# Wider projections, features by minimum, key sums halved on GpSimd, and the last key tile's causal triangle as a minimum on VectorE

## The chip, the cores and the metric

One core of a Trainium2 chip (trn2). The metric is device time of one execution in microseconds. A core has TensorE (PE), VectorE (DVE), ScalarE (ACT), GpSimd (POOL) and SyncE (SP, which here only starts DMAs). They run their own instruction streams in order and wait for each other by semaphores.

## The reference

Four residual blocks over x [2048, 512], 32 heads of 16, all in bfloat16: A, B, A, B with the same weights twice.

```python
x = x + A(layernorm(x)); x = x + B(layernorm(x)); x = x + A(layernorm(x)); x = x + B(layernorm(x))
# A: four segments of 512 tokens, M and z summed over the segments before
a_dot = softmax(q k^T / 4 + causal mask) v          # within the segment
a_mem = (phi(q) M) / (phi(q) z + 1e-6)              # phi(t) = t + 1 where t > 0, else exp(t)
o = g * a_mem + (1 - g) * a_dot                     # g = sigmoid(beta), per head;  then o @ wo
M, z = M + phi(k)^T v, z + sum(phi(k))
# B: linear attention over all 2048 tokens, without a mask
f(t) = concat(softmax(t w_phi), softmax(-t w_phi))  # over 16 features of a head, each sign
o = (f(q) (f(k)^T v)) / (f(q) sum(f(k)) + 1e-6)     # then o @ wo
```

## The kernel before

The program is a graph of operations (`Graph.op`), each with its reads, writes and buffers. The order on every engine, the engine of those operations that may run on two, and the buffer slot of every tile come from a table written into the source (`ORDER`, read by `place`). `emit` writes the five streams in that order with the waits that the graph needs. A new graph therefore has a new table: every engine's order differs.

x stays in SBUF (`X`, 16 tiles of 128 tokens). `ln` normalises a tile: statistics on DVE (L577, L578), the root on POOL (L585, L587; for the first four tiles on ACT), the scaling on DVE (L594, L598), and a transpose, mostly by DMA.

`a_proj` works on a segment. For each of four groups of eight heads it forms K and Q (512 columns each, interleaved, L341) in one PSUM tile `D`, of which there are four, each two banks wide. K is copied to `KT` (tile name `p`), and DVE writes four masked copies of it into `pQ` (L679), which put the heads apart. The feature phi is exp(t) from PSUM on ACT, max(t, 0) (L634) and min(exp, 1) + max (L635) on DVE. V gets a column of ones (`pV`); the weight of V is scaled once by 1/(1 + exp(beta)) on POOL (L530). `pW` is V with the partition halves swapped by DMA.

`a_att` works on two query tiles of a segment. For each group of heads: score products (L326) into PSUM, exponentials on ACT (L351), value products with the exponentials as stationary operand (L326, 17 columns: 16 of V and one for the sum), division (L389, L847), and from the second segment on the memory part (L764) added (L851). Scores of the diagonal tile go to `pF`, those of the last key tile, which only the second query tile sees, to `pE`. In both the causal triangle is one more product that adds -1e9 before the exponential: `tri`, the triangle, by `two`, a doubled identity.

`b_keys` forms exp(k) and exp(-k) (1024 columns on ACT for two token tiles), sums over each head's 16 features on DVE (L945), takes reciprocals, forms V and multiplies it by them straight from PSUM (L973), and adds the products with the keys (L341, `pT`). `b_query` does the queries: denominators (L1018 to L1024), the product with the sums (L1043), the sum of the two signs (L1049), the transposed output. `out_proj` applies wo; x is added by DVE (L898), or for 12 of the 32 tiles of block B by an identity product on PE (`RES_PE`, `D<-X,ident`) with a copy back.

Of the kernel before, what the change touches and what calls it, by code (L numbers as in the profile page):

```python
# [9 lines left out]
ACT = mybir.ActivationFunctionType  # L10
# [72 lines left out]

class Op:
# [5 lines left out]
class Graph:  # L90
# [4 lines left out]
    def _touch(self, o, item, write):  # L95
        if isinstance(item, tuple):
# [201 lines left out]
class Kernel:  # L298
# [97 lines left out]
    def alloc(self):  # L396
# [8 lines left out]
        self.eps6 = sb("eps6", [128, 1], F32)  # L405
        self.two64 = sb("two64", [128, 2, 64], BF16)
# [6 lines left out]
        self.gt = sb("gt", [128, 3, H], F32)  # L413
        self.GAm = sb("GAm", [128, NG, 8, 17], F32)
# [17 lines left out]
        self.pQ = pool("pQ", N_KM, [128, 4, 2, 2, 128], BF16, {}, ("KM",))  # L432
        self.pK = pool("pK", N_QT, [128, 512], BF16, {}, ("QT",))
# [16 lines left out]
    def setup(self):  # L450
# [26 lines left out]
        load(lambda: [(self.beta_sb[:], inp["A_beta"].partition_broadcast(128))], 8, [R("beta")], "pool")  # L477
        load(lambda: [(self.wphi_st[:], inp["B_w_phi"].rearrange("(g hl) d j -> (hl d) g j", g=NG))], 60, [R("wphi")], "pool")
# [34 lines left out]
        for hf in range(2):  # L513
            v(lambda e, hf=hf: e.tensor_copy(self.tri[64 * hf:64 * hf + 64, :], tw.t[64 * hf:64 * hf + 64, 64 * hf:64 * hf + 64]), 100,
              [tw], [R("tri", hf)])
        v(lambda e: e.memset(self.epsln[:], LN_EPS), 70, [], [R("epsln")])
# [4 lines left out]
        v(lambda e: e.tensor_scalar(gt[:, 1, :], gt[:, 0, :], 1.0, None, op0=ALU.add), 100, [R("gt")], [R("gt1")])  # L521
        v(lambda e: e.reciprocal(gt[:, 2, :], gt[:, 1, :]), 270, [R("gt1")], [R("gt2")])
        v(lambda e: e.tensor_tensor(self.GAm[:, :, :, 0:16], gt[:, 0, :, None].to_broadcast([128, H, 16]).rearrange("p (g h) c -> p g h c", g=NG),
                                    self.H8[:, None, :, None].to_broadcast([128, NG, 8, 16]), ALU.mult), 620,
          [R("gt"), R("H8")], [R("GAm")], label="gates")
        v(lambda e: e.tensor_copy(self.GAm[:, :, :, 16], self.H8[:, None, :].to_broadcast([128, NG, 8])), 100,
          [R("H8")], [R("GAm")], label="gates")

        for dt in range(4):
            fn = lambda e, dt=dt: e.tensor_tensor(self.WA["v"][:, dt, :].rearrange("p (h d) -> p h d", h=H),  # L530
                                                  self.WA["v"][:, dt, :].rearrange("p (h d) -> p h d", h=H),
                                                  gt[:, 2, :, None].to_broadcast([128, H, DH]), ALU.mult)
            self.g.op({"dve": (602.0, fn), "pool": (1100.0, fn)}, [R("gt2"), R("WA", "v")], [R("WAv", dt)], label="gate")

        two = lambda fn, a, b: self.g.op({"pool": (a, fn), "dve": (b, fn)}, [], [], label="one", port=True)
        for i, tv in enumerate(self.pV.tensors):
            self.pV.init[i] = two(lambda e, tv=tv: e.memset(tv[:, :, :, 16:17], 1.0), 560.0, 190.0)
# [36 lines left out]
    def ln(self, t, xT, flex=False, pe=False, root="pool"):  # L574
# [15 lines left out]
        if flex:  # L590
            nb = self.nb[:, t:t + 1]
            v(lambda e: e.scalar_tensor_tensor(nb, self.mv[:, t, 0:1], -1.0, rs, op0=ALU.mult, op1=ALU.mult), 70,
              [R("mv", t), R("rstd", t)], [R("nb", t)], label="nb")
# [35 lines left out]
    def phi(self, ps, dst, src=None, c=0):  # L629

        v = self.v
        e_ = self.T(self.p1, "phe")
        self.act(lambda: e_.t[:], lambda: ps.t[:, c:c + 512], ACT.Exp, 512, [ps[c]], [e_], label="phexp")
        v(lambda e: e.tensor_scalar(dst.t[:], src.t[:], 0.0, None, op0=ALU.max), 202, [src], [dst], label="phmax", port=True)  # L634
        v(lambda e: e.scalar_tensor_tensor(dst.t[:], e_.t[:], 1.0, dst.t[:], op0=ALU.min, op1=ALU.add), 335, [dst, e_], [dst], label="phadd", port=True)  # L635


# [20 lines left out]
    def a_proj(self, L, s):  # L658
# [7 lines left out]
        for g in range(NG):  # L666
            ps = self.T(self.pD, "gen")
            if L == 0 and s == 0 and g == 0:
                self.warm()
            KT = self.T(self.p1, "KT")  # L670
            KM = self.T(self.pQ, "KM")
            QT = self.T(self.pK, "QT")
            pk = self.T(self.p1, "phiKT") if s < 3 else None
            PQ = self.T(self.p1, "phiQ") if s >= 1 else None
            self.wproj(ps, (self.WA["k"], self.WA["q"]), [R("WA", "k", g // 2), R("WA", "q", g // 2)], (g, g), xT,
                       opens=[KT, QT] + ([pk] if pk else []) + ([PQ] if PQ else []), label="KQ")
            self.evac(lambda KT=KT: KT.t[:], lambda ps=ps: ps.t[:, 0:512], 512, [ps[0]], [KT], label="Kev")
            for sl in range(4):
                fn = lambda e, KM=KM, KT=KT, sl=sl: e.tensor_scalar(  # L679
                    KM.t[:, :, sl % 2, :, 64 * (sl // 2):64 * (sl // 2) + 64], KT.t[:].rearrange("p (j h k) -> p j h k", j=4, h=2),  # L680
                    self.m4[:, sl:sl + 1], None, op0=ALU.mult)
                self.g.op({"dve": (262.0, fn)}, [KT, R("m4")], [KM[sl]], label="Km", port=True)
            st["KM"].append(KM)
            if pk:
                PK = self.T(self.p1, "PhK")
                self.phi(ps, pk, KT)
                dst = lambda PK=PK: PK.t[:].rearrange("p (a b) -> p a b", a=4)
                if first:
                    self.tpe(dst, lambda pk=pk: pk.t, [pk], [PK], label="PhKtr")
                else:  # L690
                    self.tr(dst, lambda pk=pk: pk.t[:], [pk], [PK], label="PhKtr")
                st["PhK"].append(PK)
            self.evac(lambda QT=QT: QT.t[:], lambda ps=ps: ps.t[:, 512:1024], 512, [ps[512]], [QT], label="Qev")
            st["QT"].append(QT)
            if PQ:
                self.phi(ps, PQ, QT, 512)
                st["PhQ"].append(PQ)
        wv = lambda dt: self.WA["v"][:, dt, :].rearrange("p (k a e) -> p a k e", k=8, a=2)
        for t2 in (0, 2):
            ps = self.T(self.pD, "gen")  # L700
            self.tproj(ps, wv, [R("WAv", i) for i in range(4)], (t2, t2 + 1), lambda tt, dt: xT.t[:, dt, tt * 128:(tt + 1) * 128],
# [66 lines left out]
    def a_att(self, L, s, i0):  # L768
# [11 lines left out]
        for gg in range(2):  # L780
            PV = self.T(self.pD, "pv")
            for g in (2 * gg, 2 * gg + 1):
                KM, QT = st["KM"][g], st["QT"][g]
                rd = [QT] + [KM[sl] for sl in range(4)]
                key = lambda hf, j, p, x, KM=KM: KM.t[64 * hf:64 * hf + 64, j, p, x, :]
                qry = lambda hf, c, n, QT=QT: QT.t[64 * hf:64 * hf + 64, i0 * 128 + c:i0 * 128 + c + n]
                PT, PF = {}, {}
                for j in range(i0 + 1):
# [19 lines left out]
                    (S.t[:, hf * 512 + p * 192 + 64 * (1 - x):hf * 512 + p * 192 + 192 - 128 * x], key(hf, i0 + 1, p, x), qry(hf, 128 + 64 * x, 128 - 64 * x), p + x == 0, False)  # L808
                    for p in range(2) for x in range(2) for hf in range(2)] + [
                    (S.t[:, hf * 512:hf * 512 + 384].rearrange("p (a b) -> p a b", a=2)[:, :, 0:128], two(hf), tri(hf, 4), False, True) for hf in range(2)],  # L810
                    [], rd + trir, [S], opens=[PE], label="Sd", rows=64, dur=286)
                self.act(lambda PE=PE: PE.t[:, :, 64:256], lambda S=S: S.t[:, :].rearrange("p (a b) -> p a b", a=2)[:, :, 0:384].rearrange("p a (c e) -> p a c e", c=2),
                         ACT.Exp, 768, [S], [PE], scale=0.25, label="expd")

# [35 lines left out]
            if s >= 1:  # L850
                v(lambda e, part=part: e.tensor_tensor(part(o), part(o), part(tmp), ALU.add), 335, [o[gg], tmp], [o[gg]], label="oadd", port=True)  # L851
# [70 lines left out]
    def b_keys(self, L, c, parts):  # L922
# [4 lines left out]
        for part in parts:  # L927
            Es, Vts = {}, {}
            units = [part[i:i + 2] for i in range(0, len(part), 2)]
            for u in units:  # L930
# [9 lines left out]
                for sgn in range(2):  # L940
# [3 lines left out]
                             ACT.Exp, 512 * n, [S[0], S[512]][:n], [E[sgn]], scale=1.0 - 2.0 * sgn, label="kexp")  # L944
                    fn = lambda e, sgn=sgn, eo=eo, Z=Z, n=n: e.tensor_reduce(Z.t[:, 0:64 * n].rearrange("p (k s h) -> p k s h", k=n, s=2)[:, :, sgn, :],  # L945
# [11 lines left out]
                if copied:  # L957
# [4 lines left out]
                    for k, tt in enumerate(u):  # L962
                        Vt = Vts[tt]
                        for sgn in range(2):
                            v(lambda e, sgn=sgn, Vt=Vt, vs=vs, k=k: e.tensor_tensor(
                                Vt.t[:, sgn, :, 0:16, :], vs.t[:, k * 512:(k + 1) * 512].rearrange("p (g d h) -> p g d h", g=NG, h=8),
                                Vt.t[:, sgn, :, 16:17, :].to_broadcast([128, NG, 16, 8]), ALU.mult), 335,
                              [vs, Vt[("z", sgn)]], [Vt[("v", sgn)]], label="Vt", port=True)
# [18 lines left out]
    def b_query(self, L, c, store):  # L987
# [13 lines left out]
        zv = lambda s, k: ZQ.t[:, :].rearrange("p (a x) -> p a x", a=2)[:, :, 0:256].rearrange("p a (s k x) -> p a s k x", s=2, k=2)[:, :, s, k, :]  # L1001
# [7 lines left out]
        zr = [ZQ[(gp, sgn)] for gp in range(2) for sgn in range(2)]  # L1009
# [6 lines left out]
        self.act(lambda: u(0), lambda: zv(1, 1), ACT.Ln, 128, zr, [t1[0]], label="zln")  # L1016
# [9 lines left out]
        for tt in range(4):  # L1026
# [21 lines left out]
            if not pair:  # L1048
              v(lambda e, Tm=Tm, o=o: e.tensor_tensor(o.t[:].rearrange("p (a c) -> p a c", a=2), half(Tm, 0), half(Tm, 1), ALU.add), 335, [Tm], [o], label="nadd", port=True)  # L1049
# [8 lines left out]
    def build(self):  # L1058
# [5 lines left out]
        def lnA(L, s):  # L1064
            self.xA[(L, s)] = self.T(self.pX, "xA")
            for t in range(s * 4, s * 4 + 4):
                self.ln(t, self.xA[(L, s)], flex=(L == 1), pe=("xA", L, t) in PE_T, root="act" if L == 0 and s == 0 else "pool")
# [44 lines left out]
N_XT, N_KM, N_K1, N_K2, N_VT, N_SM, N_QT, N_PE, N_PF = 5, 6, 16, 19, 5, 6, 6, 2, 3  # L1112
# [116 lines left out]
```

## Time and profile before

| | before |
|---|---|
| median of 3 runs | 483.18 us (480.74 to 484.05) |
| profiled execution | 480.2 us, span 478.5 us, clock 0.987 |
| busy PE / DVE / ACT / POOL | 95% / 92% / 90% / 12% |

The span is the time from the first to the last instruction of the execution that was profiled. A PE record contains a fixed part beside its streaming, so records overlap and a busy PE is not at its peak. Groups of instructions are named by line, engine and operation, written tile <- read tiles; `p` and `pS` stand for the shared SBUF tiles, `D` for PSUM. A mean duration contains the start of an instruction, which overlaps the one before.

### The profile page before, as it was taken

Reading aid. Unit: us, or ns where it says so; the run is one execution under the profiler, and the core shown is the slowest. Engines: PE = TensorE matmul, PEld = TensorE weight load, DVE = VectorE, ACT = ScalarE, POOL = GpSimd, SP = SyncE. Lnnn points to the kernel's source line nnn. Section 1 sums busy time; section 2 is a strip of 40 time slices with the busy share of each in tenths; the row PEclk is TensorE's granted clock in tenths of the full one; section 3 lists DMA queues with packets and bytes.
Section 4 is the critical chain, followed back from the end, with each engine's and each line's share of the span. In section 5 each row is a group of like instructions: output and inputs, shape, how many; then the busy total and the mean of one; then the engine's idle time right before and its main releaser. Section 6 shows DMA issues by size and latency. Waiting matters only on the chain.

```text
span 478.5 us, 25222 instructions
## 1 busy us (share of the span) xinstructions
PE 454.4 (95%) x11582; PEld 300.5 (63%) x11582; DVE 438.2 (92%) x917; ACT 429.2 (90%) x566; POOL 58.2 (12%) x142
## 2 busy tenths in 40 slices
PE   7999999999999989998999998999999999999895
PEld 3456565757666776666555767676667666666453
DVE  5999999999999989898999999999999998998893
ACT  3799999999999997579999999999999999667892
POOL 2703030200011011100220020210010011110000
PEclk9999999999999999998999999999999999999799
DMA  8562433351536011200233344325113303200346
GB/s 243 142 130 54 72 71 63 76 108 32 60 65 71 20 37 25 47 1 5 36 79 79 62 68 71 57 47 95 27 26 60 47 15 60 37 12 3 47 81 209
DMA packets 89450, 30.36 MB, mean 63 GB/s; under 512 B 76000, under 2 KB 89344, under 8 KB 89344
## 3 DMA queue, kind: packets, MB, share of 16 engines
q1 hardware_dynamic: 88992, 28.46, 31.7%
q8 instruction: 91, 1.49, 1.3%
q10 hardware_dynamic: 288, 0.26, 0.2%
q0 software_dynamic: 64, 0.02, 0.1%
q14 instruction: 15, 0.12, 0.1%
HBM read 6.32 MB, written 2.10 MB: 18 GB/s over the span
## 4 chain that ended last, share of the span: by engine, by line
PE 56%; ACT 30%; DVE 9%; DMA 2%; issue 2%; POOL 1%; DVEq 0%; POOLq 0%
PE D L341 37%; PE D L326 18%; ACT p L351 15%; ACT pF L351 10%; ACT pE L351 4%; DVE stats L577 1%; DMA beta_sb<-in_A_beta_dram 1%; DVE p L764 1%; DVE pQ L679 1%; DVE p L598 1%; DMA p<-p 1%; DVE p L360 1%; PE D L378 1%; ACT pS L351 1%; DVE p L635 1%
## 5 line engine op out<-in xcount | busy, mean ns | idle before, releaser
L351 ACT ACTIVATE p<-D 128x1024 bf16<-128x1024 f32 (+1 forms) x276 | 250.2, 955 | 18.3 <-PE D L341 12.1
L326 PE MATMUL D<-pK,pQ 64*128 64x256 bf16 (+3 forms) x1536 | 114.6, 244 | 6.6 <-ACT p L351 2.8
L351 ACT ACTIVATE pF<-D 128x896 bf16<-128x896 f32 x128 | 117.1, 941 | 2.7 <-PE D L326 2.2
L326 PEld LDWEIGHTS D<-pK,pQ 64*128 64x128 bf16 x1536 | 53.8, 94 | 42.7 <-ACT p L351 11.3
L326 PE MATMUL D<-pV,pF 64*128 64x34 bf16 x1024 | 75.8, 176 | 1.9 <-ACT pF L351 1.1
L326 PE MATMUL D<-pW,pF 64*128 64x34 bf16 x1024 | 73.1, 176 | 0.0
L341 PE MATMUL D<-pX,WA_k 64*128 64x512 bf16 x256 | 65.0, 377 | 0.0
L341 PE MATMUL D<-pX,WA_q 64*128 64x512 bf16 x256 | 65.0, 377 | 0.0
L326 PEld LDWEIGHTS D<-pV,pF 64*128 64x128 bf16 x1024 | 56.2, 93 | 4.7 <-ACT pF L351 2.3
L585 POOL TENSOR_SCALAR rstd<-mv 128x1 f32<-128x1 f32 x60 | 14.6, 244 | 360.2 <-DVE mv L578 358.1
L351 ACT ACTIVATE pE<-D 128x768 bf16<-128x768 f32 x64 | 52.7, 835 | 1.4 <-PE D L326 0.7
L326 PE MATMUL D<-pV,p 64*128 64x34 bf16 x1024 | 52.8, 176 | 0.1
L326 PEld LDWEIGHTS D<-pW,pF 64*128 64x128 bf16 x1024 | 52.2, 93 | 0.8
L326 PE MATMUL D<-pW,p 64*128 64x34 bf16 x1024 | 51.5, 176 | 0.0
L326 PEld LDWEIGHTS D<-pV,p 64*128 64x128 bf16 x1024 | 47.2, 93 | 3.2 <-ACT pE L351 0.3
L326 PEld LDWEIGHTS D<-pW,p 64*128 64x128 bf16 x1024 | 45.5, 93 | 2.5
L326 PE MATMUL D<-tri,two 64*128 64x128 bf16 (+1 forms) x384 | 46.6, 234 | 0.0
L577 DVE BATCH_NORM_STATS2 stats<-X 128x6 f32<-128x512 bf16 x64 | 43.2, 683 | 3.0 <-DMA X<-in_A_x_dram 2.7
L326 PE MATMUL D<-pV,pE 64*128 64x34 bf16 x512 | 45.2, 176 | 0.2 <-issue 0.2
L326 PE MATMUL D<-pW,pE 64*128 64x34 bf16 x512 | 43.3, 176 | 0.0
L679 DVE TENSOR_SCALAR pQ<-p,m 128x512 bf16<-128x512 bf16 x128 | 42.5, 351 | 0.2
L945 DVE TENSOR_REDUCE pS<-p 128x64 f32<-128x1024 bf16 (+1 forms) x36 | 39.0, 1090 | 1.0 <-ACT p L351 1.0
(121 smaller groups left out, 1003.7 us busy)
## 6 DMA issues: line engine op xcount, KB each, us to landing
pW<-pV SPq DMA_DIRECT2D x16, 136.0 KB, 2.6
out_dram<-X SPq DMA_DIRECT2D x7, 256.0 KB, 4.4
X<-in_A_x_dram SPq DMA_DIRECT2D x3, 512.0 KB, 7.1
pX<-in_B_wqkv_dram SPq DMA_DIRECT2D x3, 512.0 KB, 5.5
p<-p SPq DMA_TRANSPOSE x76, 2.5
pX<-p SPq DMA_TRANSPOSE x54, 3.0
WA_q<-in_A_wq_dram SPq DMA_DIRECT2D x2, 256.0 KB, 6.1
WB_o<-in_B_wo_dram SPq DMA_DIRECT2D x8, 64.0 KB, 3.1
```

Source lines behind the costliest of these rows:

```text
L326: ins = e.matmul(out_ap, lhsT, rhs, start=st, stop=sp, tile_position=(basep(lhsT), basep(out_ap)))
L341: ins = e.matmul(out_ap, lhsT[64 * hf:64 * hf + 64], rhs[64 * hf:64 * hf + 64], start=k == 0 and i == 0, stop=k == 1 and i == len(lists[hf ...
L351: return self.g.op({"act": (dur, lambda e: e.activation(out_ap(), in_ap(), func, scale=scale))}, reads, writes, opens, label=label)
L360: "dve": ((340 if fast else n / 0.96 + 65), lambda e: e.tensor_copy(out_ap(), in_ap()))}
L378: ins = e.transpose(pb()[:, k * 128:(k + 1) * 128], src()[:, k * 128:(k + 1) * 128], self.ident[:])
L577: v(lambda e: e.bn_stats(self.stats[:, t, :], self.X[:, t, :]), 602, [R("X", t)], [R("st", t)], label="bn")
L585: v(lambda e: e.tensor_scalar(rs, self.mv[:, t, 1:2], LN_EPS, None, op0=ALU.add), 170, [R("mv", t)], [R("rstd", t)], eng="pool", label="rstd")
L598: v(lambda e: e.tensor_scalar(xn.t[:], self.X[:, t, :], self.mv[:, t, 0:1], self.rstd[:, t:t + 1], op0=ALU.subtract, op1=ALU.mult), 300, [ ...
L635: v(lambda e: e.scalar_tensor_tensor(dst.t[:], e_.t[:], 1.0, dst.t[:], op0=ALU.min, op1=ALU.add), 335, [dst, e_], [dst], label="phadd", po ...
L679: fn = lambda e, KM=KM, KT=KT, sl=sl: e.tensor_scalar(KM.t[:, :, sl % 2, :, 64 * (sl // 2):64 * (sl // 2) + 64], KT.t[:].rearrange("p (j h ...
L764: v(lambda e: e.tensor_tensor(tmp.t[:].rearrange("p (y h r d) -> p y h r d", y=16, h=2, r=2), NM.t[:, :].rearrange("p (h y r d) -> p y h r ...
L945: fn = lambda e, sgn=sgn, eo=eo, Z=Z, n=n: e.tensor_reduce(Z.t[:, 0:64 * n].rearrange("p (k s h) -> p k s h", k=n, s=2)[:, :, sgn, :], eo( ...
```

## The change

- **Projections.** K of two groups (1024 columns) fills a PSUM tile, then Q of the two; copies, masks and features work on 1024 columns. `pQ` and `pK` have half as many tiles of double size; the other pools change in number.
- **Features.** phi = min(exp(t), max(t, 0) + 1); exp reads the copy in SBUF, not PSUM.
- **Gates.** V's weight is no longer scaled. V's extra column is 1 + exp(beta), and the mask of the memory is scaled in place of it.
- **Key sums.** GpSimd halves 16 features to 8 and 8 to 4; DVE sums 4. This is done for the units of two token tiles (28 sums); the 8 of single tiles stay.
- **Values and denominators of B** are copied from PSUM to SBUF first, and the multiplication makes both signs in one instruction.
- **Residual.** All additions of x are on DVE.
- **Triangle.** For `pE` the product with `tri` is gone; after the exponential DVE takes the minimum with `keep`, which is 3e38 where a key is seen and 0 where not. `pF` keeps its product.
- Two sums (L851, L1049) may run on POOL (9 and 16 of 50 do). The loads of beta and w_phi go to the queues of ACT and SP.
- A new order table.

```diff
...
-        self.pQ = pool("pQ", N_KM, [128, 4, 2, 2, 128], BF16, {}, ("KM",))
-        self.pK = pool("pK", N_QT, [128, 512], BF16, {}, ("QT",))
+        self.pQ = pool("pQ", N_KM, [128, 8, 2, 2, 128], BF16, {}, ("KM",))
+        self.pK = pool("pK", N_QT, [128, 1024], BF16, {}, ("QT",))
...
+            fn = lambda e, tv=tv: e.tensor_copy(tv[:, :, :, 16], self.gc[:, None, :].to_broadcast([128, 4, H]))
...
-        self.act(lambda: e_.t[:], lambda: ps.t[:, c:c + 512], ACT.Exp, 512, [ps[c]], [e_], label="phexp")
-        v(lambda e: e.tensor_scalar(dst.t[:], src.t[:], 0.0, None, op0=ALU.max), ...
-        v(lambda e: e.scalar_tensor_tensor(dst.t[:], e_.t[:], 1.0, dst.t[:], op0=ALU.min, op1=ALU.add), ...
+        self.act(lambda: e_.t[:], lambda: src.t[:], ACT.Exp, 1024, [src], [e_], psum=False, label="phexp")
+        v(lambda e: e.tensor_scalar(dst.t[:], src.t[:], 0.0, 1.0, op0=ALU.max, op1=ALU.add), ...
+        v(lambda e: e.tensor_tensor(dst.t[:], e_.t[:], dst.t[:], ALU.min), ...
...
+            self.wproj(ps, (self.WA["k"],) * 2, [R("WA", "k", hp)], gs, xT, opens=[KT], label="KQ")
+            self.evac(lambda KT=KT: KT.t[:], lambda ps=ps: ps.t[:], 1024, [ps[0], ps[512]], [KT], label="Kev")
...
-                    (S.t[:, hf * 512:hf * 512 + 384].rearrange("p (a b) -> p a b", a=2)[:, :, 0:128], two(hf), tri(hf, 4), False, True) for hf in range(2)],
...
+                v(lambda e, PE=PE: e.tensor_tensor(PE.t[:, :, 64:192].rearrange("p a (b c) -> p a b c", b=2), PE.t[:, :, 64:192].rearrange("p a (b c) -> p a b c", b=2),
+                                                   self.keep[:, None, None, :].to_broadcast([128, 4, 2, 64]), ALU.min), 335, ... label="cutd", port=True)
...
+                        self.g.op({"pool": (1160.0, lambda e, e3=e3, s3=s3: e.tensor_tensor(s3(), e3()[:, :, 0:8], e3()[:, :, 8:16], ALU.add))},
+                                  [E[sgn]], [sc], label="zh")
+                        self.g.op({"pool": (770.0, lambda e, s3=s3: e.tensor_tensor(s3()[:, :, 0:4], s3()[:, :, 0:4], s3()[:, :, 4:8], ALU.add))},
+                                  [sc], [sc], label="zh")
...
-N_XT, N_KM, N_K1, N_K2, N_VT, N_SM, N_QT, N_PE, N_PF = 5, 6, 16, 19, 5, 6, 6, 2, 3
+N_XT, N_KM, N_K1, N_K2, N_VT, N_SM, N_QT, N_PE, N_PF = 5, 3, 10, 21, 5, 6, 3, 2, 4
...
-VCOP = set()
+VCOP = {(L, c) for L in range(2) for c in range(4)}
...
-RES_PE = {(0, t) for t in (2, 3, 6, 7)} | {(1, t) for t in (2, 3, 6, 7, 10, 11, 14, 15)}
+RES_PE = set()
...
```

More of the change, by code (lines that the diff above doesn't have):

```diff
@@ L81, in t, with __init__ @@
         return self.pool.tensors[self.slot]
+class Half:
+    __slots__ = ("tile", "k")
+    def __init__(self, tile, k):
+        self.tile = tile
+        self.k = k
+    @property
+    def t(self):
+        return self.tile.t[:, 512 * self.k:512 * self.k + 512]
 class Op:
@@ L526, in setup @@
[L526 to L533, printed above, removed]
+        v(lambda e: e.tensor_scalar(self.gc[:].rearrange("p (a k r) -> p a k r", a=2, r=2), gt[:, 0, :].rearrange("p (k a r) -> p a k r", a=2, r=2), 1.0, None, op0=ALU.add),
+          100, [R("gt")], [R("gc")])
@@ L683, in a_proj @@
-            st["KM"].append(KM)
+                self.g.op({"dve": (400.0, fn)}, [KT, R("m4")], [KM[sl]], label="Km", port=True)
+            for k in range(2):
+                st["KM"].append((KM, 4 * k))
             if pk:
[L685 to L692, printed above, removed]
```

245 lines of the change are left out of this document (141 added, 104 removed).

## The prediction

> **What bounds the kernel now.** I read the page first, then a table of seven stretches of the span, then the chain inside each stretch, then the groups. The page's busy rows, the chain by engine and the table (columns: length, busy us with instructions of TensorE, weight loads, VectorE, ScalarE and GpSimd, then granted clock and DMA):
>
> ```profile
> span 478.5 us, 25222 instructions
> PE 454.4 (95%) x11582; PEld 300.5 (63%) x11582; DVE 438.2 (92%) x917; ACT 429.2 (90%) x566; POOL 58.2 (12%) x142
> ...
> PE 56%; ACT 30%; DVE 9%; DMA 2%; issue 2%; POOL 1%; DVEq 0%; POOLq 0%
> ```
>
> ```profile
> 0.00:36.00 36.00, 31.91 (x388) 16.14 (x390) 29.94 (x79) 24.33 (x42) 11.50 (x30) 1.00 0.66 172
> 36.00:180.00 144.00, 139.17 (x4086) 96.68 (x4084) 135.52 (x274) 141.30 (x180) 17.10 (x40) 1.00 0.37 60
> 180.00:216.00 36.00, 35.94 (x740) 22.83 (x738) 33.54 (x57) 25.58 (x31) 3.23 (x8) 1.00 0.11 24
> 216.00:240.00 24.00, 21.50 (x598) 14.66 (x591) 21.35 (x57) 22.99 (x39) 3.56 (x8) 0.93 0.14 20
> 240.00:408.00 168.00, 163.31 (x4512) 112.17 (x4510) 158.91 (x342) 165.01 (x211) 19.62 (x48) 1.00 0.32 56
> 408.00:432.00 24.00, 23.96 (x444) 14.81 (x440) 23.73 (x42) 16.24 (x20) 3.21 (x8) 1.00 0.16 25
> 432.00:478.50 46.50, 38.59 (x846) 23.24 (x842) 35.25 (x72) 33.72 (x50) 0.00 (x0) 0.90 0.37 87
> ```
>
> Three engines are nearly full at once. In the two attention stretches (36 to 180, 240 to 408) ScalarE is 98% busy, TensorE 97%, VectorE 94%. At 180 to 216 and 408 to 432 TensorE alone is full, and ScalarE has slack. So no engine's saving reaches the end one for one; I weight each saving by the share that its engine has in the chain of its stretch. Chains by line, for 0 to 36, 36 to 180, 240 to 408 and 432 to the end:
>
> ```profile
> by line: DMA beta_sb<-in_A_beta_dram 14.0%; DVE pQ L679 11.5%; DVE stats L577 10.1%; DVE p L598 10.0%; ACT p L351 8.4%; ACT pF L351 6.7%; issue 6.0%; PE D L341 5.3%; DVE p L360 3.5%; DVE p L635 3.3%; DVE pV L360 3.0%; PE D L326 2.4%; DVE mv
> by line: ACT p L351 25.9%; ACT pF L351 18.8%; PE D L341 18.6%; PE D L326 16.3%; ACT pE L351 7.3%; DVE p L764 2.5%; issue 1.6%; DVE p L635 1.0%; DVE pK L360 0.8%; DVE p L360 0.8%; DVE pS L945 0.8%; DVE p L851 0.8%; ACT WB_v L359 0.7%; ACT p
> by line: PE D L341 40.1%; PE D L326 28.7%; ACT p L351 11.9%; ACT pF L351 10.7%; ACT pE L351 4.5%; DMA p<-p 2.4%; issue 0.9%; DVE p L764 0.7%; ACT pS L751 0.2%; DVEq L275 0.0%
> by line: PE D L341 60.1%; PE D L326 12.0%; ACT p L351 10.8%; issue 3.1%; ACT pS L351 1.6%; ACT X L359 1.3%; PE D L867 1.2%; ACT p L359 1.1%
> ```
>
> The head is VectorE's; the first attention stretch is 52% ScalarE and 35% TensorE; the second is 69% TensorE; the tail is 73% TensorE. VectorE, although 92% busy, is on 7% of the first stretch and 1% of the second.
>
> **The change, part by part. TensorE.** The triangle of the last key tile was one product of 256 columns in each half of the array, 64 pairs of them; the identity products that added X to the output are gone too (20 of 512 columns, and in the program 8 of 256).
>
> ```profile
> L326 PE MATMUL D<-tri,two 64*128 64x256 bf16 x128 | 17.9, 270 | 0.0
> L326 PE MATMUL D<-Rz,p 64*128 64x8 bf16 x512 | 8.0, 164 | 1.6 <-DVE Rz L918 0.8 <-issue 0.8
> L341 PE MATMUL D<-pX,WA_q 64*128 64x512 bf16 x256 | 65.0, 377 | 0.0
> L341 PE MATMUL D<-X,ident 64*128 64x512 bf16 x20 | 3.9, 378 | 0.0
> ```
>
> A record holds a fixed part; the 8-column row is nearly that alone (164 ns). So 256 columns stream for 270 - 164 = 106 ns, 512 for 213, and two halves run together. The triangle: 64 x 0.106 = 6.8 us, half in each attention stretch: 3.4 x 0.35 + 3.4 x 0.69 = **3.5 us** of the end (bounds 0 and 6.8). X: 10 x 0.213 + 4 x 0.108 = 2.6 us, of which 1.7 in the tail: 1.7 x 0.73 + 0.9 x 0.69 = **1.8 us** (bounds 0 and 2.6).
>
> **VectorE**, where most edits fall (rows picked from the groups, the costliest first):
>
> ```profile
> L679 DVE TENSOR_SCALAR pQ<-p,m 128x512 bf16<-128x512 bf16 x128 | 42.5, 351 | 0.2
> L945 DVE TENSOR_REDUCE pS<-p 128x64 f32<-128x1024 bf16 x28 | 33.7, 1209 | 1.0 <-ACT p L351 1.0
> L973 DVE TENSOR_TENSOR pT<-D,pT 128x1024 bf16<-128x1024 f32 x28 | 33.5, 1215 | 3.0 <-PE D L341 2.8
> L635 DVE SCALAR_TENSOR_TENSOR p<-p 128x512 bf16<-128x512 bf16 x48 | 32.4, 683 | 0.6
> L898 DVE TENSOR_TENSOR X<-X,D 128x1024 bf16<-128x1024 bf16 x23 | 27.9, 1218 | 4.3 <-PE D L341 4.1
> L1043 DVE TENSOR_TENSOR p<-p,pS 128x1024 bf16<-128x1024 bf16 x32 | 21.6, 686 | 2.4 <-ACT p L351 2.1
> L360 DVE CAST pK<-D 128x512 bf16<-128x512 f32 x25 | 17.1, 684 | 1.0 <-PE D L341 0.9
> L360 DVE CAST pV<-D 128x1024 bf16<-128x1024 f32 x11 | 13.3, 1212 | 0.7 <-PE D L341 0.7
> L851 DVE TENSOR_TENSOR p<-p 128x512 bf16<-128x512 bf16 x24 | 9.9, 417 | 0.3
> L634 DVE TENSOR_SCALAR p<-p 128x512 bf16<-128x512 bf16 x24 | 6.8, 285 | 0.1
> L945 DVE TENSOR_REDUCE pS<-p 128x32 f32<-128x512 bf16 x8 | 5.3, 672 | 0.0
> ```
>
> Two SBUF tensors take 417 ns at 512 elements and 686 at 1024, so 148 ns are fixed.
> - Key masks: 128 of 512 become 64 of 1024. One costs between 351 + (285 - 148) = 488 and 2 x 351 = 702 ns; I take 520, since the 285 row shows the same kind of operation streaming at that rate. 44.9 becomes 33.3: -12.
> - Features: 48 maxima of 285 become 24 of about 422, 48 additions of 683 become 24 minima of 686: 46.5 becomes 26.6: -20.
> - Key sums: 28 reductions of 1209 shrink to 256 elements, 672 - (1209 - 672)/2 = 404 ns: -22.5. The two halvings go to GpSimd.
> - Value products now read a copy in SBUF: 28 of 1215 become 28 of 686, and 8 of about 0.4 merge into 4 of 686: -15.
> - PSUM copies: fewer but longer, plus 9 of the value copies and 5 of the denominators: +11 by the 684 and 1212 rows. Residual adds from ScalarE and the dropped identity products, +5 of 1218 and +2 of about 0.67: +7.
> - 25 of 50 sums move to GpSimd at 417: -10.
> - New: 64 minima for the triangle, 512 elements, two SBUF tensors with one repeated: 417 each (bounds 285, and 683 as L635 has it): +27.
>
> Sum -35, before what GpSimd does to it. That is the doubtful term.
>
> **GpSimd** gets 56 halvings and 25 sums. The only comparable work before is the weight gating, and it shows a cost to VectorE:
>
> ```profile
> L530 POOL TENSOR_TENSOR WA_v<-WA_v,gt 128x512 bf16<-128x512 bf16 x4 | 4.8, 1208 | 0.0
> 17.98 1.46 POOL L530 TENSOR_TENSOR WA_v<-WA_v,gt 128x512 bf16<-128x512 bf16 x1
> 18.45 1.14 DVE L598 TENSOR_SCALAR p<-X,mv,rstd 128x512 bf16<-128x512 bf16 x1
> 19.51 1.67 DVE L679 TENSOR_SCALAR pQ<-p,m 128x512 bf16<-128x512 bf16 x2
> ```
>
> (Rows of the timeline of either engine: start, duration, engine, what.) The normalisation at 18.45 ends with the GpSimd instruction, and takes 1.14 us, where most take 0.41; two masks take 1.67, not 0.70. That is 1.7 us of stall for 4.8 us of GpSimd, 0.35 us per us. Added: 28 first halvings and 25 sums at 1.21, 28 second ones at about 0.7 (half the elements; bounds 0.2 and 1.21), less the gating's 4.8: 79 us. At 0.35 this is 28 us. But in the changed program's order 58 of the 81 have as next VectorE instruction one that reads PSUM, a statistic or a reduction, kinds that show no such stretching here; drift will spoil some of that. I take 0.2: 16 us (bounds 0 and 79). VectorE then is 20 us lighter, about 6 of them in the first stretch; with VectorE on 7% of that chain (10 us), 6/135.5 of it is **0.4 us**.
>
> The Trainium skill speaks against this part: "SBUF — State Buffer", section "SBUF: two separate sides", says that GpSimd and those VectorE instructions that use its second port, or have two SBUF inputs, hold a common port pair exclusively for a whole instruction. The rows at 18.45 and 19.51 agree; by the rule alone all 79 us could be stall.
>
> **ScalarE.** 48 exponentials of 512 from PSUM become 24 of 1024 from SBUF.
>
> ```profile
> L351 ACT ACTIVATE p<-D 128x1024 bf16<-128x1024 f32 x220 | 220.6, 1043 | 14.5 <-PE D L341 10.0 <-PE D L326 3.2
> L351 ACT ACTIVATE p<-D 128x512 bf16<-128x512 f32 x56 | 32.4, 609 | 3.8 <-PE D L341 2.1 <-DVE p L360 0.9 <-DVE pK L360 0.5
> L351 ACT ACTIVATE pS<-pS 128x128 f32<-128x128 f32 x22 | 6.8, 319 | 0.6 <-DVE pS L1021 0.4
> L351 ACT ACTIVATE pS<-D 128x128 f32<-128x128 f32 x8 | 2.3, 293 | 0.0
> PEld D L326 <- ACT pE L351: 4.4, 15, 0.6
> PE D L326 <- ACT pE L351: 1.2, 4, 0.4
> ```
>
> Reading SBUF adds 26 ns, so 29.2 becomes 24 x 1.07 = 25.7: -3.5 us; copies leave and enter in equal amounts. At ScalarE's 52% and 27% of the two chains this is **1.3 us** (bounds 0 and 3.5).
>
> **The new wait.** The triangle's minimum stands between the exponential and the value products. Before, TensorE met a late exponential of that tile in 19 cases, 5.6 us in all (last two rows above: us in total, times, longest). In each the minimum now adds at least its 0.417: 7.9 us. The new order puts more groups of products between the scores and the first value product that needs them (median 12, was 9.5), which hides most: I take **+3 us** (bounds 0, and 64 x 0.417 = 27). VectorE executes in order: behind a minimum that waits for ScalarE stand PSUM copies and statistics, and for the copies waits TensorE, which has four double banks.
>
> **The head.** K and Q of one group ran interleaved; now two groups of K go first, then Q. The first score waits 1.7 us more for products (8 pairs of 0.213), 0.4 for a copy of 1024 instead of 512, 0.35 for wider masks: +2.5. But VectorE carries the chain up to 27 us, and loses there some 3.4 us of masks and features and the 1.7 us of stall under the gating, which is gone: **-2.7 us** (bounds -5, +2.5). The beta load moves from GpSimd's queue to ScalarE's, behind one X load; its exponential now stands behind two roots, so they do not wait for it. The w_phi load goes to SyncE's queue, 16 KB among the weights, hidden by the transfers after it. Larger and fewer buffers hold the same bytes, and PSUM no longer waits for the feature exponentials: nothing counted (bounds -3, +3).
>
> **Sum:** -3.5 - 1.8 - 0.4 - 1.3 + 3 - 2.7 = -6.7 us. The profiled execution took 480.2 (span 478.5, 1.7 around it): 473.5. The median shown is 483.18, 3.0 higher: 476.5. I predict between the two, **475 us**.
>
> **Rivals.**
> *TensorE takes the whole saving* (chance 0.27). If the lighter VectorE frees banks earlier, the stretches close up until TensorE is the bound: 478.5 - 9.4 - 2.7 = 466.4, time 468. For it: ScalarE's waits before its 1024-column group are on TensorE (10.0 + 3.2 us above). Against it: ScalarE is at 98% in attention, and keeps its work.
> *Nothing arrives* (0.17). ScalarE sets the attention stretches, the triangle's 3.5 is absorbed and the new wait eats the rest: 480.2 - 1.8 - 1.3 + 3 = 480, or 483 by the median.
> *VectorE is locked out by GpSimd* (0.10). VectorE idles 20 us in head, change-over and tail in any case. If stall is 0.85 per us of GpSimd, it is 67, and VectorE has 438 - 35 + 67 = 470 busy: 490 span, 492. It decides from about 0.7 on (438 - 35 + 55 + 20 = 478). Against it: the order avoids most meetings.
> *The minimum comes late* (0.08). If all 64 show, with TensorE on half of the chain, it costs 14 instead of 3: 480.2 - 9.7 + 14 = 484.5, or 487 by the median.
>
> **How the numbers follow.** The forecast has 0.38, with an own range of 469 to 481. This kernel's runs spread by 0.7%, so about 1% can be told from no change. Faster by over 1% (under 478.4): 0.31 of the forecast and the first rival, 0.58. Within 1%: 0.07 of the forecast, most of the second rival and half of the last, 0.25. Slower: the lock and the rest, 0.17. The range runs from the first rival with buffers helping (461) to near the lock (489).
>
> **What would show it.** Right: triangle products only for 64x128, minima near 0.42 us, reductions near 0.40, feature minima near 0.69, VectorE busy near 419, TensorE near 445 and ScalarE near 426. Wrong: masks or minima whose mean is half again above these (the lock), TensorE waiting for VectorE's pE over 8 us in all, the first scores after 19 us, or a chain with over 20% VectorE.

## The result, and the profile after

The changed kernel takes **496.2 us** (median, 495.1 to 497.7) where the kernel before took 482.0 beside it (480.7 to 484.1): ratio 1.029, 95% interval 1.025 to 1.034. It is slower; 475 and "faster" were predicted. The profiled execution took 497.7, with a span of 496.0. The page's busy rows and its chain by engine:

```profile
span 496.0 us, 24883 instructions
PE 451.8 (91%) x11426; PEld 292.7 (59%) x11426; DVE 436.0 (88%) x840; ACT 430.1 (87%) x538; POOL 141.6 (29%) x221
...
PE 40%; DVE 30%; ACT 25%; DMA 2%; issue 2%; POOL 0%; ACTq 0%; DVEq 0%
```

Apart from GpSimd no engine is busy more than 1 us longer than before, and yet each is idle for longer: TensorE is busy 451.8 us (454.4 before), VectorE 436.0 (438.2), ScalarE 430.1 (429.2). So the loss is in how they wait for each other, and VectorE's share of the chain went from 9% to 30%. By stretches (columns as in the table of before):

```profile
36.00:180.00 144.00, 134.88 (x4062) 93.59 (x4058) 131.93 (x246) 138.63 (x168) 37.41 (x56) 1.00 0.38 64
...
240.00:408.00 168.00, 156.05 (x4168) 104.06 (x4170) 151.08 (x290) 154.79 (x186) 51.58 (x76) 0.97 0.29 52
```

In attention TensorE and ScalarE, 97 and 98% busy before, are at 94 and 96% in the first of these and at 93 and 92% in the second. Rows picked from the groups: what the prediction priced, and what is new on GpSimd:

```profile
L340 PE MATMUL D<-tri,two 64*128 64x128 bf16 x256 | 28.6, 217 | 0.0
L697 DVE TENSOR_SCALAR pQ<-p,m 128x1024 bf16<-128x1024 bf16 x64 | 33.3, 542 | 1.6 <-ACT p L373 1.3
L838 DVE TENSOR_TENSOR pE<-pE,keep 128x512 bf16<-128x512 bf16 x64 | 29.3, 466 | 4.0 <-ACT pE L365 3.9
L1003 DVE TENSOR_TENSOR pT<-p,pT 128x1024 bf16<-128x1024 bf16 x32 | 25.6, 819 | 1.9 <-ACT p L373 1.6
L618 DVE TENSOR_SCALAR p<-X,mv,rstd 128x512 bf16<-128x512 bf16 x44 | 22.7, 519 | 3.5 <-POOL rstd L607 3.5
L655 DVE TENSOR_TENSOR p<-p 128x1024 bf16<-128x1024 bf16 x24 | 17.5, 727 | 0.3
L980 DVE TENSOR_REDUCE pS<-p 128x64 f32<-128x256 f32 x28 | 11.1, 407 | 2.9 <-POOL p L978 2.9
L612 DVE SCALAR_TENSOR_TENSOR nb<-mv,rstd 128x1 f32<-128x1 f32 x20 | 5.6, 292 | 0.2 <-ACT rstd L603 0.2
L976 POOL TENSOR_TENSOR p<-p 128x512 f32<-128x512 bf16 x28 | 33.8, 1206 | 86.3 <-ACT p L365 75.8 <-DVE p L877 4.6 <-PE D L340 4.1
L978 POOL TENSOR_TENSOR p<-p 128x256 f32<-128x256 f32 x28 | 22.6, 810 | 1.6
L1090 POOL TENSOR_TENSOR p<-p 128x512 bf16<-128x512 bf16 x16 | 20.4, 1275 | 71.8 <-DVE p L1084 71.8
L877 POOL TENSOR_TENSOR p<-p 128x512 bf16<-128x512 bf16 x9 | 11.4, 1271 | 28.9 <-DVE p L873 23.2 <-DVE p L789 5.8
```

The means hide two kinds of instruction. The timeline of GpSimd and of VectorE at two places (start, duration, engine, what) shows them apart:

```profile
87.24 1.26 POOL L877 TENSOR_TENSOR p<-p 128x512 bf16<-128x512 bf16 x1 [3.67 <-DVE p L789]
87.41 0.41 DVE L980 TENSOR_REDUCE pS<-p 128x64 f32<-128x256 f32 x1
87.74 1.05 DVE L654 TENSOR_SCALAR p<-p 128x1024 bf16<-128x1024 bf16 x1
...
234.61 1.15 POOL L1090 TENSOR_TENSOR p<-p 128x512 bf16<-128x512 bf16 x1
234.66 1.12 DVE L612 SCALAR_TENSOR_TENSOR nb<-mv,rstd 128x1 f32<-128x1 f32 x1
...
236.30 0.14 DVE L612 SCALAR_TENSOR_TENSOR nb<-mv,rstd 128x1 f32<-128x1 f32 x1
```

While the sum on GpSimd runs, the reduction takes its usual 0.41 us, but the maximum that starts next takes 1.05 and ends only after the sum has. The bias of one number per partition takes 1.12 us beside a sum, and 0.14 when nothing runs there. Call this stretching; summed up, it is the time of each VectorE instruction above the median of the faster half of its kind, from 0.1 us on: 28.6 us in some 40 instructions, 2.2 us in the kernel before. Theory **L**: it is the loss. Rivals: **C**, the 64 minima (29.3 us of VectorE, and a link behind the exponential); **O**, the new order with its wider projections; **Q**, not the traffic but the delay: GpSimd's queue, which also holds the roots of the normalisation, and results that come later.

### The profile page after: what moved, and what is told of

It reads as the page before. It is cut to its first block, busy times and chain, and to the rows that moved or that the text cites. A ratio compares the mean times of both kernels' runs of the same rounds, so it can differ in the third digit from the quotient of the medians.

```text
span 496.0 us, 24883 instructions
## 1 busy us (share of the span) xinstructions
PE 451.8 (91%) x11426; PEld 292.7 (59%) x11426; DVE 436.0 (88%) x840; ACT 430.1 (87%) x538; POOL 141.6 (29%) x221
## 4 chain that ended last, share of the span: by engine, by line
PE 40%; DVE 30%; ACT 25%; DMA 2%; issue 2%; POOL 0%; ACTq 0%; DVEq 0%
PE D L355 26%; ACT p L365 12%; PE D L340 12%; ACT pF L365 7%; ACT pE L365 4%; DVE X L925 3%; DVE p L1084 3%; DVE pT L1003 2%; DVE stats L597 2%; DVE pQ L697 2%; DVE p L374 2%; DVE p L618 2%; DVE p L873 2%; DVE pE L838 1%; DMA X<-in_A_x_dram 1%
## 5 line engine op out<-in xcount | busy, mean ns | idle before, releaser
L365 ACT ACTIVATE p<-D 128x1024 bf16<-128x1024 f32 (+1 forms) x228 | 224.1, 1027 | 19.0 <-PE D L340 9.5
L340 PE MATMUL D<-pK,pQ 64*128 64x256 bf16 (+3 forms) x1536 | 112.0, 244 | 10.9 <-ACT pF L365 2.3
L605 POOL TENSOR_SCALAR rstd<-mv 128x1 f32<-128x1 f32 x60 | 15.8, 266 | 152.1 <-DVE mv L598 152.0
L976 POOL TENSOR_TENSOR p<-p 128x512 f32<-128x512 bf16 x28 | 33.8, 1206 | 86.3 <-ACT p L365 75.8
L340 PEld LDWEIGHTS D<-pW,p 64*128 64x128 bf16 x1024 | 44.1, 93 | 1.3
L925 DVE TENSOR_TENSOR X<-X,D 128x1024 bf16<-128x1024 bf16 (+1 forms) x36 | 39.1, 1092 | 5.7 <-PE D L355 5.3
L340 PE MATMUL D<-pV,pE 64*128 64x34 bf16 x512 | 44.0, 175 | 0.0
L1090 POOL TENSOR_TENSOR p<-p 128x512 bf16<-128x512 bf16 x16 | 20.4, 1275 | 71.8 <-DVE p L1084 71.8
L607 POOL TENSOR_TENSOR rstd<-rstd,mhalf 128x1 f32<-128x1 f32 x60 | 35.9, 604 | 3.7
L355 PE MATMUL D<-WB_o,p 64*128 64x512 bf16 (+1 forms) x288 | 34.7, 367 | 2.1 <-DMA p<-p 1.1
```

What stands on the lines that cost most here:

```text
L340: ins = e.matmul(out_ap, lhsT, rhs, start=st, stop=sp, tile_position=(basep(lhsT), basep(out_ap)))
L355: ins = e.matmul(out_ap, lhsT[64 * hf:64 * hf + 64], rhs[64 * hf:64 * hf + 64], start=k == 0 and i == 0, stop=k == 1 and i == len(lists[hf ...
L365: return self.g.op({"act": (dur, lambda e: e.activation(out_ap(), in_ap(), func, scale=scale))}, reads, writes, opens, label=label)
L605: v(lambda e: e.tensor_scalar(rs, self.mv[:, t, 1:2], LN_EPS, None, op0=ALU.add), 170, [R("mv", t)], [R("rstd", t)], eng="pool", label="rstd")
L607: v(lambda e: e.tensor_tensor(rs, rs, self.mhalf[:], ALU.pow), 540, [R("rstd", t), R("mhalf")], [R("rstd", t)], eng="pool", label="rstd")
L925: self.v(lambda e: e.tensor_tensor(X(), X(), src(), ALU.add), 65 + 512 * n / 0.96, pr + xr, xr, label="res")
```

## The experiments

All times are medians; the kernel before took 481.2 to 482.0 beside them. The last two columns are the busy time (us) of VectorE and of GpSimd in the profile. x2, x3, x5, x6, y1, v1 to v3 and w1 leave out part of the sums (the expectations say which part); the others do the whole computation.

| run | us | ratio to before (95%) | VectorE | GpSimd |
|---|---|---|---|---|
| changed kernel | 496.2 | 1.029 (1.025-1.034) | 436.0 | 141.6 |
| x1 sums on VectorE | 497.5 | 1.032 (1.029-1.036) | 433.7 | 111.0 |
| x2 no halvings | 483.8 | 1.003 (1.001-1.006) | 420.8 | 86.0 |
| x3 both | 484.9 | 1.007 (1.003-1.010) | 417.6 | 55.3 |
| x4 triangle products | 492.0 | 1.021 (1.017-1.025) | 415.4 | 142.9 |
| x5 halvings as idle time | 483.8 | 1.005 (1.003-1.007) | 421.0 | 133.6 |
| x6 halvings, result unread | 494.4 | 1.028 (1.025-1.030) | 436.4 | 142.5 |
| x9 all on VectorE | 498.3 | 1.034 (1.032-1.037) | 438.8 | 54.9 |
| x7 = x9, triangle products | 497.7 | 1.034 (1.031-1.036) | 419.2 | 54.3 |
| v2 no sums on GpSimd | 484.2 | 1.005 (1.003-1.007) | 424.8 | 117.3 |
| v1 = x2 and v2 | 472.7 | 0.983 (0.980-0.987) | 409.0 | 61.6 |
| v3 = v1, sums as idle time | 471.5 | 0.978 (0.972-0.983) | 409.3 | 90.6 |
| w1 = v1, triangle products | 476.4 | 0.989 (0.987-0.991) | 390.1 | 61.6 |
| w2 first halvings twice | 513.0 | 1.065 (1.062-1.068) | 447.0 | 177.2 |
| c1 before, with minima | 515.8 | 1.072 (1.068-1.076) | 459.6 | 58.9 |
| c2 before, minimum features | 480.5 | 0.999 (0.996-1.001) | 426.6 | 57.3 |
| c3 before, unread halvings | 502.4 | 1.044 (1.039-1.048) | 446.6 | 108.2 |
| y1 = x3, identity products back | 490.1 | 1.017 (1.012-1.022) | 412.8 | 55.2 |

**Take GpSimd's new work away, or the minima (x1 to x4).** The order table stays as it is, but for instructions that are gone.

```diff
-  oadd, nadd: 25 on GpSimd
+  oadd, nadd: on VectorE, in the same places                                  (x1, x3)
-  zh: s3 = e3[:, :, 0:8] + e3[:, :, 8:16]; s3[:, :, 0:4] += s3[:, :, 4:8]     (GpSimd)
-  Zred4: tensor_reduce(Z, s3[..., 0:4])
+  Zred4: tensor_reduce(Z, E[..., 0:4])                                        (x2, x3)
-  cutd: tensor_tensor(PE, PE, keep, min)                                      (VectorE)
+  Sd: two more products two64 x tri, as before                                (x4)
```

> The changed kernel with its 25 sums (9 of the memory part, 16 of the query part) on VectorE again, the 56 halvings still on GpSimd. Theory L (GpSimd's instructions stretch VectorE's while both run, 28.6 us in all, and 17 of the 28.6 reach the end): 12 us of stretching go, 25 x 0.417 = 10.4 us of work come, so about 495 us, no change within 1%. Theory C (the 64 triangle minima are what costs, GpSimd is harmless): 10.4 us more on VectorE at 0.6 give 502. Theory O (the coarser projections with the new order): 496.

> The changed kernel without the 56 halvings on GpSimd: the reductions read 4 of each 16 features from the exponentials instead of the halved sums (as many elements, 256), so three quarters of each key sum are left out. GpSimd loses 56 us of work, VectorE's instructions stay the same in number and size. Theory L: 16 us of stretching go, at 0.6 that is 10 us, so 486 us. Theory C: 496. Theory O: 494 to 496.

> Both: no halvings (three quarters of each key sum left out) and the 25 sums on VectorE, so that GpSimd does nothing that the kernel before did not do. Theory L: stretching falls from 28.6 to under 3 us, work rises by 10.4, net -16, at 0.6 about 486 us, with VectorE's busy time near 420. Theory C: 496 to 502. Theory O: 496.

> The changed kernel with the causal triangle of the last key tile as products on TensorE again and the 64 minima on VectorE gone; everything else, GpSimd's work too, as in the changed kernel. Theory C: the 29 us of minima and the link behind the exponential are the loss, so 478 to 481 us. Theory L: the stretching (28.6 us) stays, but VectorE is 29 us lighter, which gives it back part: 484 to 488, with stretching unchanged. Theory O: 494 to 500.

x2 gains 12.4 us though VectorE's 840 instructions are the same in number and size: they take 15.2 us less. C falls: without the minima (x4) VectorE is 20.6 us lighter, and 4.2 us are gained where C said 15 or more. L missed there too: its stretching stayed (27.3 us), but it said 484 to 488. x1 and x3 gain nothing on their partners (the changed kernel and x2), as L said: 10.4 us of work came for 11 to 12 of stretching. O would have given x1 the same; it fails on x2 and x3, for which it said 494 to 496.

**Traffic or delay (x5, x6).** x5 keeps GpSimd's queue and the reduction's wait, with instructions that move one number per partition; x6 keeps the traffic and takes the wait.

```diff
+  zh: pow(eps6, mhalf) three times into one column each; Zred4 reads E[..., 0:4], waits for zh     (x5)
+  zh as it is, into a buffer nobody reads; Zred4 reads E[..., 0:4]                                 (x6)
```

> As the run without halvings (three quarters of each key sum left out), but each pair of halvings is replaced by three powers of one number per partition on GpSimd, 3 x 0.6 = 1.8 us instead of 2.0, in the same place of GpSimd's queue and with the reduction waiting for them as it waited for the halvings. So the delay of the queue and of the key sums stays, and the traffic of a 512-element GpSimd instruction goes. Theory L (instructions stretched while both engines move data): 484 us as without halvings, VectorE's stretch about 13 us. Theory Q (the roots of the normalisation behind 56 us of halvings in GpSimd's queue, and the key sums later by 2 us each): 494 to 497.

> The halvings run on GpSimd as in the changed kernel, but nothing reads their result: the reductions read 4 of each 16 features from the exponentials (three quarters of each key sum left out). Theory L: the stretch stays at 28 us, so 494 to 497 us. Theory Q, the part that says the key sums come later: 484. Theory Q, the part that says the roots come later: 494 to 497 (told from L by the run with powers).

The groups of x5 show that the time on GpSimd is there:

```profile
L974 POOL TENSOR_TENSOR p<-eps,mhalf 128x1 f32<-128x1 f32 x84 | 48.2, 592 | 88.3 <-ACT p L365 66.2 <-DVE pV L374 9.1 <-DVE p L877 4.3
```

48.2 us of GpSimd that others wait for cost nothing (483.8, as with none); 56 us of halvings that nobody reads cost 10.6 (494.4). For the halvings Q falls, and L stands.

**The other half, and the dose (v1, v2, v3, w2).** 12.7 us of stretching were left in x2, all but 0.9 of it under the 25 sums.

```diff
-  oadd, nadd on GpSimd: 512 columns
+  oadd, nadd on GpSimd: one column                               (v2; v1: and x2's edit)
+  oadd, nadd on GpSimd: pow twice, then one column, x2's edit    (v3)
+  first zh run twice                                             (w2)
```

> The run without halvings (483.8 us), and the 25 sums that GpSimd does shrunk to one column each, in their places (three quarters of each key sum and 511 of 512 columns of these sums left out). GpSimd then runs nothing long, VectorE does exactly what the changed kernel planned for it: about 408 busy, stretching under 2 us. Theory L for the whole loss: the remaining 12 us of stretching reach the end at 0.6 to 0.8: 474 to 477 us, which is the forecast of 475. Theory O (wider projections and new order lose): 481 to 484.

> The changed kernel with its halvings, and the 25 sums on GpSimd shrunk to one column each (511 of 512 columns of these sums left out). Stretching 28.6 to about 17 us. Theory L: 12 x 0.6 to 0.8 less, 487 to 489 us. Theory O: 494 to 496.

> The changed kernel with each of the 28 first halvings run twice on GpSimd (same input, same output), 34 us more on GpSimd, the key sums 1.2 us later. Theory L at 0.34 us of stretch for each us (11.5 for 33.8): stretching 28.6 to about 40, and 0.78 of it arrives: 504 to 506 us. If the loss were a fixed price of the order: 496 to 498.

> As the run with neither halvings nor sums on GpSimd (472.7 us; same parts left out), but each of the 25 sums is replaced by two powers of one number per partition (2 x 0.6 us) and the sum of one column, in the same place of GpSimd's queue with the same waits on both sides. The delay of a sum stays, the traffic of a 512-element instruction goes. Theory L: 471 to 475 us. Theory Q (the later result and the queue cost): 481 to 484, as with the sums themselves.

v1's busy rows and chain, and the groups that were stretched:

```profile
span 467.9 us, 24818 instructions
PE 442.0 (94%) x11426; PEld 290.8 (62%) x11426; DVE 409.0 (87%) x840; ACT 426.7 (91%) x538; POOL 61.6 (13%) x165
...
PE 42%; ACT 41%; DVE 11%; DMA 3%; issue 1%; ACTq 0%; POOL 0%; DVEq 0%
```

```profile
L697 DVE TENSOR_SCALAR pQ<-p,m 128x1024 bf16<-128x1024 bf16 x64 | 29.8, 488 | 0.3
L838 DVE TENSOR_TENSOR pE<-pE,keep 128x512 bf16<-128x512 bf16 x64 | 25.9, 414 | 4.8 <-ACT pE L365 4.7
L997 DVE TENSOR_TENSOR pT<-p,pT 128x1024 bf16<-128x1024 bf16 x32 | 21.1, 678 | 3.2 <-ACT p L373 2.9
L618 DVE TENSOR_SCALAR p<-X,mv,rstd 128x512 bf16<-128x512 bf16 x44 | 17.7, 404 | 3.5 <-POOL rstd L607 3.5
L612 DVE SCALAR_TENSOR_TENSOR nb<-mv,rstd 128x1 f32<-128x1 f32 x20 | 2.7, 150 | 0.2 <-ACT rstd L603 0.2
```

The same 840 instructions of VectorE take 409.0 instead of 436.0, and the kernel 472.7 instead of 496.2: 27.0 us of stretching cost 23.5, or 0.87 each. v3 says that it is not the sums' delay: two powers (0.62 to 0.64 us each) and a short sum in each place, 471.5. So the loss is not a fixed price of the new order (O). v1 and v2 came out 1 and 3 us under what L said. w2 goes the other way: its stretching is 39.9 us, as said, but 11.0 us more of VectorE cost 16.8 of time, above what L said. GpSimd itself is on 7% of that chain, so there part of it may be delay.

Stretching is not dearer than other time, though. x3 and v1 differ in where the 25 sums run, and have 0.9 us of stretching each; VectorE's 8.6 us more in x3 cost 12.2 us (484.9 against 472.7). x1 and v2, with 17.6 and 17.2 us of stretching, differ in the same way: 8.9 us cost 13.3. In this order, VectorE time beyond the plan cost between 0.6 (x9, below) and 1.5 us per us, whatever it was made of.

**What the minima cost, and VectorE's work (w1, x9, x7, c1).** 

```diff
-  cutd (VectorE)
+  Sd: products two64 x tri back               (w1 on v1; x7 on x9)
-  zh, zh, Zred4 of 256; sums on GpSimd
+  Zred of 1024; sums on VectorE               (x9)
-  Sd: products two64 x tri
+  cutd, two ScalarE instructions behind expd  (c1, kernel and order of before)
```

> The run with neither halvings nor sums on GpSimd (same parts left out), and the triangle as products on TensorE again: VectorE 29 us lighter, TensorE about 6.8 us of streaming heavier. It prices the minima where nothing is stretched. Prediction's terms (-3.5 for the products, +3 for the wait): the same time within 1 us. If TensorE bounds then: 2 to 6 us slower than with minima. If VectorE bounds: 4 or more faster.

> The whole computation with nothing moved to GpSimd: full reductions of 1024 elements (1.21 us) on VectorE instead of halvings and short reductions, and the 25 sums on VectorE; the rest as in the changed kernel, the minima too. Against the run without halvings and with the sums on VectorE (484.9 us) it adds 28 x 0.8 = 22.5 us to VectorE (418 to 440 busy). Theory L with VectorE setting the chain where GpSimd met it (0.6 to 0.8 of each us arrives): 495 to 500. Theory that only stretched instructions at a few bad places hurt: 486 to 490.

> As the run before it, and the triangle as products on TensorE, without the 64 minima: what is left of the change are the wider projections, the minimum features, the copied value products and the residual adds. VectorE 440 - 29 = 411 busy, TensorE 7 us more. If the minima cost what they cost in the changed kernel (4 us): 4 us under the run with all on VectorE. If they cost more with VectorE the fuller engine: 10 to 15 under it, near 481. If the new order alone loses (theory O): 486 or more.

> The kernel before, in its own order, with one part of the change alone: the triangle of the last key tile as 64 minima on VectorE (0.42 to 0.47 us each, 27 to 30 us) and 128 products of 256 columns off TensorE (6.8 us of streaming), each minimum two ScalarE instructions behind its exponential in the order. If the minima are as good as free, as the two runs with everything on VectorE say (498.3 with them, 497.7 without): 480 to 482 us. If VectorE, with 438 + 28 = 466 busy, is too full for them: 488 to 492. If the prediction's term was right (-3.5 and +3): 481.

Where nothing is stretched and VectorE is light, the minima gain 3.7 us (476.4 to 472.7), as expected if TensorE bounds; it is on 57% of w1's chain. In the changed kernel itself they cost 4.2 (x4). x9 against x3: 21 us more of reductions in places planned for short ones cost 13.4. x7 takes 20 us off VectorE, gives TensorE the triangle back and gains 0.6. Its 497.7 lies where its expectation put O (486 or more): with nothing on GpSimd and without the minima, the rest of the change in its order is 16 us slower than the kernel before, though VectorE has 19 us less to do. So an order made for short key sums doesn't carry long ones well, and v1's gain is seen only with part of the work left out. And c1, which all three expectations missed, takes 515.8: VectorE's queue comes to a minimum as the old order has its place, and TensorE waits, by the waits of c1 (us in total, times, longest) and then of the changed kernel:

```profile
PEld D L326 <- DVE pE L820: 19.1, 17, 3.3
PE D L326 <- DVE pE L820: 17.7, 17, 3.0
```

```profile
PEld D L340 <- DVE pE L838: 2.4, 3, 1.4
PE D L340 <- DVE pE L838: 2.0, 2, 1.3
```

What makes the minima so much dearer in c1 than in the new order, the old order itself or a fuller VectorE (459.6 us busy, 436.0 in the changed kernel), c1 does not separate. It has one placing only; a better one in the old order wasn't tried.

**The same edits in the order of before (c2, c3), and the residual adds (y1).** 

```diff
-  dst = max(x, 0); dst = min(e, 1) + dst
+  dst = max(x, 0) + 1; dst = min(e, dst)             (c2)
+  zh, zh into free buffers, one ScalarE instruction behind the exponential   (c3)
-  RES_PE = set()
+  RES_PE = the 12 tiles of before                    (y1, on x3)
```

> The kernel before with the features alone as min(exp, max+1): 48 instructions of 683 ns become 48 of 417, 12.8 us less on VectorE, nothing else moved, order and operands as before. By the prediction's weight (VectorE on 7% of the chain): 1 us, 480 us. By the weight that the runs without the halvings show (0.6 to 0.8 of each us): 471 to 474 us. So this says whether VectorE's work set the end of the kernel before.

> The kernel before, whole computation, with the 56 halvings run on GpSimd beside it and their result read by nobody (into buffers that are free at the time). VectorE's work is unchanged. Theory L, general: 16 to 20 us of stretching, at 0.6 to 0.8 of each us 492 to 496 us. Theory L, but only where VectorE already sets the chain, as in the changed order: stretching of 16 us and 481 to 486 us. No lock: 481.

> The run without halvings and with the sums on VectorE (484.9 us; three quarters of each key sum left out), with the identity products that add X to the output on TensorE back at the old places: residual adds off VectorE (about 7 us; 6 of the copies to ScalarE), 2.6 us more on TensorE. It asks what the other 3 to 4 us above the kernel before are, though VectorE is 20 us lighter there. Theory R (the residual adds on VectorE, above all at the change of layers): 479 to 482. Theory O (wider projections and the new order, above all at the change of layers): 484 to 486.

c2 takes 11.6 us off VectorE and gains 1.4 (by the interval, between 1.8 gained and 0.3 lost): VectorE's own work did not set the end, as the prediction had it. c3 costs 20.5, more than L gave, though its stretching is less than L gave: 9.9 us, 7.7 more than before for 50 us of GpSimd, 0.15 per us. VectorE is 8.4 us longer, and in the waits GpSimd's queue stands at halvings that wait for exponentials, and the normalisation (L598) waits for roots (L587) of the same queue (0.5 us before):

```profile
POOL p L952 <- ACT p L351: 68.0, 11, 11.6
...
DVE p L598 <- POOL rstd L587: 11.8, 6, 3.1
```

These waits speak for Q where the order doesn't know of the halvings; no run with idle time in place of the halvings tested it there. y1 missed both expectations: it is 5.2 us slower than x3, so the residual adds on VectorE are no loss; why the copies that replace them cost so much is open. v1, v3 and w1 are faster than the kernel before, all three with work left out; of the runs that do the whole computation none is by what the measurement can tell, c2 being nearest.

## Why the prediction was wrong

- **The step that failed is the one on GpSimd,** "I take 0.2: 16 us", and its weight in the end, 0.4 us with all of VectorE. The row it rested on gave 0.35 us per us; measured are 27.0 us of stretching for 88.2 us of GpSimd (33.8 + 22.6 + 20.4 + 11.4), 0.31. The discount was argued from what stands next in the order; that the engines drift apart at run time is a likely reason, not shown.
- **The weight was the larger error.** VectorE's share of the old chain (7%) was used for time that is lost. For work taken off VectorE in the old order that is about right (c2: 11.6 us, 1.4 gained). For stretching it is 0.87, and for the sums that x3 puts on VectorE beyond v1 it is 1.4: with the stretching VectorE is on 30% of the chain, in v1 on 11%. By the row's own 0.35 and the weight 0.87, known only from v1, about 79 x 0.35 x 0.87 = 24 us would have been added, and about 499 forecast.
- **The rest of the sum held as a total,** in part by luck. Without the stretching the kernel takes 472.7 and 471.5, where the sum gave 473.5 to 476.5 and the forecast was 475. v1 gains 8.6 on the kernel before, where 6.7 were said: 3.7 from the triangle and its wait, where 0.5 was said, and 4.9 from all else, where 6.2 was. The terms for the head, for X and for ScalarE were not measured apart. Busy times in v1: TensorE 442.0 (said 445), ScalarE 426.7 (426), VectorE 409.0 (438 - 35 = 403). Masks are 488 ns, the lower bound (520 taken); key sums 407 (404), value products 678 (686), minima 414 (417).
- **The triangle and its wait:** -3.5 and +3 were said, -3.7 measured for both (w1 against v1). The wait is not there in v1 (0.2 us) and is 4.4 us in the changed kernel. There the minima as a whole cost 4.2 (x4), probably because their own time comes on a VectorE that already holds up the others.
- **The rival "locked out by GpSimd"** had the mechanism, 492 us, and a chance of 0.10. It failed in its point of decision, 0.7 us per us, since it let stall fill VectorE's idle time first. At 0.31 the stall already cost 23.5 of 27.0 us: the idle time took up little of it.
- **The marks.** The chain (over 20% VectorE) spoke as it should. The first scores came at 19.7 us, after 19, but that marked nothing: in x6 (494.4 us) and w2 (513.0) they came at 17.7 and 18.3. "Half again above" for masks and minima did not (542 and 466): the mean over 64 dilutes a few that triple.

## What to carry to other kernels

Price work moved to GpSimd by what it does to the other engine's instructions while it runs, and weigh that by what waits for them (here 0.87), not by the share of an engine in the old chain. Work taken off an engine and time put on it are not the same coin: in this order 19 to 21 us off VectorE, with the triangle back on TensorE, gave between 4.2 us gained (x4) and 3.7 lost (w1), while 8.6 us put on it cost 12.2. An edit that loads an engine should be judged with the order and the fullness that it meets: the minima gained 3.7 us with VectorE at 409 us, cost 4.2 in the changed kernel, and 34 in the old order with one placing.

## What the runs showed of the hardware

- Which VectorE instructions GpSimd holds: those that read SBUF with two tensors, or with one at a fast rate (normalisation: 512 elements in 0.40 us, where statistics take 0.68): masks, maxima, minima, products, and even one number per partition (1.12 us instead of 0.14). Reductions, statistics, reciprocals, copies from PSUM, and sums and products with one input in PSUM keep their time. Counted in the changed kernel, for those that began beside a halving or a sum with over 0.3 us still to run: 33 of 34 of the first kinds were lengthened by 0.1 us or more, and 0 of 37 of the second. The Trainium skill, "SBUF — State Buffer", section "SBUF: two separate sides", says that these two engines hold a common port pair in turn, each for a whole instruction; the rows at 87.74 and 234.66 agree.
- GpSimd's powers of one number per partition, 0.59 us each, hold nothing that shows: 48.2 us of them left VectorE at 421.0 (420.8 without), and of 41 instructions of the kinds above that began beside a power in x5 none was lengthened. The section of the Trainium skill named above excepts no such GpSimd instruction; here the measurement goes against it.
- The mean granted TensorE clock does not tell the changed kernel from the one before: 0.979 to 0.990 over its four executions, 0.981 to 0.990 over those of the kernel before. It was 0.981 to 0.996 in v1, and lowest in the slowest runs (0.958 to 0.971 in c1, 0.969 to 0.972 in w2). The same 11426 products took 442.0 us in v1's profile (clock 0.996) and 451.8 in the changed kernel's (0.979). How much of the 23.5 us goes by way of the clock was not separated.
